# Rows in natural order, one x transfer a group, and an output product merged with the next group's value product in a convolution kernel

## The chip, the cores and the metric

The kernel runs on one core of a Trainium2 chip. The metric is device time in microseconds (us) of one execution; lower is better. A core has five engines that run side by side and wait for one another by semaphores: PE (TensorE, the matmul array, whose weight loads the profile lists as PEld), DVE (VectorE), ACT (ScalarE), POOL (GpSimd) and SP (SyncE). SP and POOL also issue the DMA transfers here; all of these run on the core's 16 DMA engines.

## What is computed

The reference, cut to what matters (batch 8, sequence 4224, 192 channels, 8 heads of 24 channels):

```python
w = softmax(weight_gen)                      # (8, 4224, 8 heads, 7 taps)
x_pad = concat([zeros(8, 6, 192), x], 1)
x_unf = x_pad[:, idx, :].reshape(B, S, 7, 8, 24)
y = einsum('bshk,bskhg->bshg', w, x_unf)     # a convolution with its own 7 taps at every row and head
y = y.reshape(B, S, 192)
gate_pre = sum(conv_w[k] * y_pad[:, k:k + S, :] for k in range(5))   # 5 taps a channel
gate = 1 / (1 + exp(-gate_pre))
out = (gate * (y @ w_val)) @ w_out
```

## The kernel before

**Groups.** The sequence is cut into 36 groups of 118 rows (`BLK`), each for all eight batches. With the rows that the taps reach back to, a group needs 128 rows of x, one for each partition. The per-row convolution is done on PE as a product with a band matrix: for each batch and head the moving operand `tb` holds, in each of the 128 input rows, that row's weights for the output rows it reaches, and the stationary operand is that batch's and head's x. A group goes through these steps:

- `load_x` (L404 to L415): x into `xt`, three buffers. A whole group (all but the first and the last) has eight transfers on POOL's queue, one a batch, 128 rows of 768 bytes each; the first and last group load by chunks of 16 rows on SP's.
- `load_t` (L417 to L424): the softmax weights, which were stored earlier to a DRAM tensor `zd` in a sheared layout, into `tb`, two buffers, in eight chunks of 16 rows on SP's queue. Row r of chunk j lies in partition 8 r + j.
- `bank` (L426 to L441): the convolution, 64 products (128 PE instructions, since each fp32 product takes two passes) on a 32-column split of the array, in four kinds of 16 products, each kind into one PSUM tile `pa`.
- `evac` (L443 to L455): ACT copies `pa` to `A` (channels of four heads a batch), `B` and `S`.
- `move` (L457 to L466): eight small SBUF to SBUF transfers on POOL's queue put the channels of the last two heads from `S` into the holes of `A` (four, L464) and `B` (four, L466).
- `tap0`, `tap`, `sigm` (L472 to L488): the five-tap gate on ACT, DVE and ACT into `aA` and `aB`.
- `val` (L490 to L505): the value product into `v2` (a 64-column split for `A`, L497, then 128 x 128 for `B`, L499) and `v01` (128 x 128, L501, then a split by 64 rows, L504).
- `gv` (L507 to L513): DVE multiplies gate and value in place in `aA`, `aB`.
- `omm` (L515 to L540): the output product, in two halves k = 0, 1, each into the one PSUM tile `po`: a part from `aA` (128 x 128, L524) and one from `aB` (split by 64 rows, L531). Half 0 does the `aB` part first, half 1 the `aA` part.
- `oev` (L542 to L547): ACT copies `po` to `ot`; `store` (L549 to L555): two transfers on SP's queue.

The softmax itself (`Softmax`, L246 to L327) runs in ten parts on DVE and ACT, ahead of the groups that need it, so that it is mixed into about the first two thirds of the groups; its results go to `zd` in transfers of up to 12 rows a partition (L327), from the fourth part on on POOL's queue.

**What sets the order.** Every step is an operation with an engine, an estimated duration, a key (roughly, its due time in groups) and dependencies, added to `Order` (L17 to L86) by `add`. `Order.run` simulates the engines with these estimates and issues on each the open operation with the lowest key among those that could start within `SLACK` of the first. The order that comes out is the instruction order of each engine, and engines and queues go through theirs in order. PE operations carry a `mode` (the shape of the array: "32c", "64c", "64r", "128"); a change of mode costs `SWITCH` in the estimate. `deps` wait for an operation's end; `behind` only fixes the order of issue. The loop over groups (L629 to L700) adds a group's operations: a convolution needs its x and tb, and that the same PSUM buffers were copied out in the group before; the value product needs the moves and that the group before's `gv` is done; an output half needs `gv` and the copying out of the half before it.

Of the kernel before, what the change touches and what calls it, by code (L numbers as in the profile page):

```python
# [7 lines left out]
FP32 = mybir.dt.float32  # L8
# [8 lines left out]
class Order:  # L17
# [1 line left out]


    SLACK = 0.08
    SWITCH = 0.1
    SEM = 0.08
    RATE = 260e3
    LAND = {"SP": 2.8, "ACT": 2.8, "POOL": 3.8}
# [16 lines left out]
    def run(self):  # L42
        for o in self.ops:
            o.left = len(o.deps) + len(o.behind)
            for d in o.deps:
                d.users.append((o, True))
            for d in o.behind:
                d.users.append((o, False))
        free, mode, dma = {}, {}, 0.0
        open_ = {}  # L50
        for n, o in enumerate(self.ops):
            if not o.left:
                open_.setdefault(o.eng, []).append((n, o))
        number = {id(o): n for n, o in enumerate(self.ops)}
        done = 0
        while done < len(self.ops):
            best = None
            for eng, c in open_.items():
                if not c:
                    continue  # L60
                t = free.get(eng, 0.0)
                first = min(max(t, o.ready) for _, o in c)
                n, o = min(((n, o) for n, o in c if max(t, o.ready) <= first + self.SLACK), key=lambda x: (x[1].key, x[0]))
                s = max(t, o.ready)
                if best is None or s < best[0]:
                    best = (s, n, o)
            s, n, o = best
            open_[o.eng].remove((n, o))
            e = s + o.dur
            if o.mode is not None:  # L70
                if mode.get(o.eng, o.mode[0]) != o.mode[0]:
                    e += self.SWITCH
                mode[o.eng] = o.mode[-1]
            free[o.eng] = e
            o.start, o.end = s, e + self.SEM
            if o.bytes:
                dma = max(dma, e + 0.8) + o.bytes / self.RATE
                o.end = dma + self.LAND[o.eng]
# [11 lines left out]
def tile_dynconv_gated_moe(  # L90
# [9 lines left out]
    nc = tc.nc  # L100

    B, S, D = x.shape
# [3 lines left out]
    P = 128  # L106
# [17 lines left out]
    G = 16  # L124
# [255 lines left out]
    class Group:  # L380
# [12 lines left out]

        def rows(self, j):


            lo = FRONT if self.m == 0 and j == 0 else 0
            hi = min(G, self.k - G * j)
            return lo, hi, slice(NGR * lo + j, NGR * (hi - 1) + j + 1, NGR)

        def whole(self):
            return 0 < self.m < NM - 1
# [1 line left out]
        def load_x(self, j):  # L404

            r0 = self.s - FRONT
            if self.whole():
                src = bass.AP(tensor=x.tensor, offset=x.offset + (j * S + r0) * D,
                              ap=[[D, G], [G * D, NGR], [1, D]])
                nc.gpsimd.dma_start(out=self.xb[:, j, 0:D], in_=src)  # L410
# [79 lines left out]
        def val(self):  # L490
            n = HB * self.n
            v2 = self.v2 = ps_v.tile([P, 512], FP32, name="v2")
            v01 = self.v01 = ps_v.tile([P, 2, 512], FP32, name="v01")
            A, Bt = self.part(0, HALO), self.part(1, HALO)
            A = [A[:, HB * u:HB * u + HB] for u in range(2)]
            for u in range(2):
                nc.tensor.matmul(out=v2[HD * u:HD * u + HD, 0:n], lhsT=wvm, rhs=A[u], start=True, stop=False,  # L497
                                 tile_position=(0, HD * u))
            nc.tensor.matmul(out=v2[:, 0:n], lhsT=wvd, rhs=Bt, start=False, stop=True)  # L499
            for u in range(2):  # L500
                nc.tensor.matmul(out=v01[:, u, 0:n], lhsT=wva, rhs=A[u], start=True, stop=False)  # L501
            for u in range(2):
                hs = slice(HD * u, HD * u + HD)
                nc.tensor.matmul(out=v01[:, u, 0:n], lhsT=wvb[hs], rhs=Bt[hs], start=False, stop=True,  # L504
                                 tile_position=(HD * u, 0))  # L505

        def gv(self, g):  # L507
# [7 lines left out]
        def omm(self, k):  # L515

            n = self.n
            po = self.po = ps_o.tile([P, 2, 512], FP32, name="po")

            def a_part(first):  # L520
                for u in range(2):
                    for t in range(2):
                        c = n * (HB * u + 2 * k + t)
                        nc.tensor.matmul(out=po[0:n, u, D * t:D * t + D], lhsT=self.aA[:, c:c + n], rhs=woa,  # L524
                                         start=first and t == 0, stop=not first, skip_group_check=True)

            def b_part(first):
                for t in range(2):
                    for u in range(2):
                        hs, c = slice(HD * u, HD * u + HD), n * (2 * k + t)  # L530
                        nc.tensor.matmul(out=po[0:n, u, D * t:D * t + D], lhsT=self.aB[hs, c:c + n], rhs=wob[hs],  # L531
                                         start=first and t == 0, stop=not first, skip_group_check=True,
                                         tile_position=(HD * u, 0))

            if k == 0:
                b_part(True)
                a_part(False)
            else:
                a_part(True)
                b_part(False)  # L540

        def oev(self, k):  # L542
            if k == 0:
# [65 lines left out]
    def dep(m, name):  # L609
        return T[m][name] if m >= 0 else []  # L610
# [5 lines left out]
    def soft_part(i):  # L616
# [6 lines left out]
        else:  # L623
            softmax(r0, R, at - 5.5, at - 2.2, at - 7.0, at - 1.7)

    for i in range(3):
        soft_part(i)
    late_clear.behind.append(soft[1]["exp"])
    for m, gp in enumerate(gr):  # L629
        if 2 <= m < len(PARTS) - 1:  # L630
# [5 lines left out]
        old = T[m - 3]["bank"] if m >= 3 else [*xpad, xz]  # L636
        late = (() if m == 0 else T[m - 1]["loadt"]) if m < 3 else ()
        d["loadx"] = [add("POOL" if gp.whole() else "SP", 0.55, (-90, -35, -1)[m] if m < 3 else m - 2.2,
                          lambda gp=gp, j=j: gp.load_x(j), old, bytes=G * B * D * 4, behind=late)
                      for j in (range(B) if gp.whole() else gp.chunks)]  # L640
# [49 lines left out]
        d["gv"] = gv  # L690
        d["useA"], d["useB"] = [val, tp[0][-1]], [val, tp[1][-1]]
        o = []
        evs = []
        for k in range(2):
            o.append(add("PE", 6 * mm(D), m + 2.1 + 0.3 * k, lambda gp=gp, k=k: gp.omm(k),
                         [*gv, conv["o"], *(evs[-1:] if k else dep(m - 1, "oev")[-1:])], mode=(("64r", "128"), ("128", "64r"))[k]))
            evs.append(add("ACT", act(4 * D, True), m + 1.2, lambda gp=gp, k=k: gp.oev(k), [o[-1], *(lent("store") if k == 0 else [])]))
        d["out"], d["oev"] = o, evs
        d["store"] = [add("SP", 0.55, m + 2.0, lambda gp=gp, i=i: gp.store(i), evs, delay=4.0,
                          bytes=n * D * 4 * (B if i == 0 else 1)) for i in range(2)]  # L700
    od.run()


# [24 lines left out]
```

## Time and profile before

| | |
|---|---|
| median of 3 runs | 589.19 us |
| lowest, highest | 588.93, 590.83 us |
| the profiled execution's own time | 587.95 us |
| its span in the profile | 586.2 us |
| granted TensorE clock, mean over the span | 0.932 |
| moved by DMA | 123.17 MB in 105869 packets, mean 210 GB/s |

The profile is of one execution. "Busy" is the time in which an engine executes; register, semaphore and DMA-issuing work of a sequencer (SPq, POOLq) is not counted. A row of the timeline gives the start, the length, the engine, the line, the operation, output <- inputs, and how many instructions of this kind in a row (x8); in brackets stands the idle time of the engine before it and what ended it. A row of the groups by line gives the sum of busy time, the mean of one in ns, and the idle time ahead of them with what ended it. The chain that ended last is followed back from the last instruction, at each step to what released it; "issue" is time for which the profile shows no reason. Matmuls overlap with the next one, so that the starts of PE's rows tell more than their lengths. The granted clock is a share of full speed.

### The profile page before, as it was taken

The numbers are of one execution on the slowest core, as the hardware profiler recorded it, in microseconds if no ns is written. First come the engines' busy times: TensorE is split into PE (matmuls) and PEld (weight loads), VectorE is DVE, ScalarE is ACT, GpSimd is POOL, SyncE is SP. The second block draws the span as 40 slices with busy tenths as digits, with TensorE's granted clock in tenths as the row PEclk, the third lists the DMA queues.
The fourth block names the chain that finished last, engine by engine and source line by source line (L and its number), as shares of the span: only waits on it lengthen the run. The fifth ranks groups of instructions, "written<-read, shape, count | busy, mean of one in ns | idle before, by whom it ended". The sixth has DMA issues, their size and how long they took to land.

```text
span 586.2 us, 15839 instructions
## 1 busy us (share of the span) xinstructions
PE 484.9 (83%) x6278; PEld 327.0 (56%) x6278; DVE 438.5 (75%) x488; ACT 345.0 (59%) x533; POOL 330.2 (56%) x613
## 2 busy tenths in 40 slices
PE   2033868599848988999979997998999999999994
PEld 1033535386525764566746673765766675767653
DVE  6776396679857299898887889878975679667780
ACT  4435554478535667458666766586585656546641
POOL 9535956256470666657457455677576687522410
PEclk7557879799987999999979998999999999999999
DMA  5989689738799998879997989799789868775222
GB/s 156 213 239 242 144 223 257 200 99 236 216 236 228 283 266 243 207 207 246 290 259 187 267 217 275 212 261 252 194 217 259 248 158 200 205 183 164 66 60 89
DMA packets 105869, 123.17 MB, mean 210 GB/s; under 512 B 17938, under 2 KB 95615, under 8 KB 103107
## 3 DMA queue, kind: packets, MB, share of 16 engines
q1 hardware_dynamic: 79779, 65.40, 42.5%
q0 software_dynamic: 26016, 56.75, 36.1%
q8 instruction: 50, 0.82, 0.6%
q14 instruction: 24, 0.20, 0.1%
HBM read 64.55 MB, written 51.43 MB: 198 GB/s over the span
## 4 chain that ended last, share of the span: by engine, by line
PE 40%; DMA 30%; POOL 13%; issue 8%; ACT 4%; DVE 2%; SPq 1%; POOLq 0%; ACTq 0%; DVEq 0%
DMA zd<-zt 13%; PE po L524 10%; PE pa L437 10%; POOL xt L410 7%; DMA A<-S 6%; PE po L531 5%; DMA xt<-in_x_dram 5%; PE v L501 5%; DMA tb<-zd 3%; PE v L499 3%; PE v L504 3%; PE v L497 3%; POOL A L464 2%; DMA raw_c<-cd 1%; POOL B L466 1%
## 5 line engine op out<-in xcount | busy, mean ns | idle before, releaser
L483 DVE SCALAR_TENSOR_TENSOR aA<-A,wf,aA 128x944 f32<-128x944 f32 (+1 forms) x144 | 171.6, 1192 | 26.6 <-ACT aA L478 22.8
L437 PE MATMUL pa<-tb,xt 128*32 128x122 f32 (+1 forms) x4608 | 140.5, 276 | 48.8 <-DMA tb<-zd 43.1
L410 POOL DMA_DIRECT2D xt<-in_x_dram x272 | 143.8, 549 | 44.0 <-DMA A<-S 8.7
L437 PEld LDWEIGHTS pa<-tb,xt 128*32 128x32 f32 x4608 | 127.7, 110 | 64.0 <-issue 56.1
L483 DVE SCALAR_TENSOR_TENSOR aB<-B,wf,aB 128x472 f32<-128x472 f32 (+1 forms) x144 | 101.2, 703 | 46.2 <-ACT aB L478 39.0
L466 POOL DMA_DIRECT2D B<-S x144 | 74.7, 525 | 95.8 <-ACT B L451 83.5
L524 PE MATMUL po<-wf,aA 128*118 128x192 f32 (+1 forms) x576 | 117.2, 349 | 11.8 <-DVE aA L511 9.4
L524 PEld LDWEIGHTS po<-wf,aA 128*118 128x118 f32 (+1 forms) x576 | 94.6, 188 | 43.2 <-issue 20.1
L464 POOL DMA_DIRECT2D A<-S x144 | 74.2, 521 | 69.2 <-DMA zd<-zt 36.9
L546 ACT COPY ot<-po 118x768 f32<-118x768 f32 (+1 forms) x72 | 57.8, 803 | 82.3 <-PE po L531 49.4
L531 PE MATMUL po<-wf,aB 64*118 64x192 f32 (+1 forms) x576 | 68.6, 358 | 26.6 <-ACT ot L546 16.8
L531 PEld LDWEIGHTS po<-wf,aB 64*118 64x118 f32 (+1 forms) x576 | 45.8, 183 | 42.6 <-ACT ot L546 18.9
L501 PE MATMUL v<-A,wva 128*128 128x472 f32 (+1 forms) x144 | 63.6, 562 | 0.0
L455 ACT COPY S<-pa 64x488 f32<-64x488 f32 (+1 forms) x72 | 40.5, 562 | 31.1 <-PE pa L437 30.6
L488 ACT ACTIVATE aA<-aA 128x944 f32<-128x944 f32 (+1 forms) x36 | 35.5, 986 | 32.5 <-DVE aA L483 32.5
L511 DVE TENSOR_TENSOR aA<-v,aA 128x944 f32<-128x944 f32 (+1 forms) x36 | 40.7, 1130 | 13.7 <-PE v L504 8.1
L320 ACT COPY zt<-wt 128x192 f32<-128x192 f32 (+3 forms) x100 | 39.1, 461 | 17.5 <-DVE wt L308 11.4
L478 ACT ACTIVATE aA<-A,wf 128x944 f32<-128x944 f32 (+1 forms) x36 | 38.9, 1081 | 14.2 <-DMA A<-S 14.2
L501 PEld LDWEIGHTS v<-A,wva 128*128 128x128 f32 x144 | 27.7, 192 | 31.0 <-issue 30.4
L448 ACT COPY A<-pa 128x488 f32<-128x488 f32 (+1 forms) x72 | 40.5, 565 | 6.5 <-PE pa L437 5.3
L497 PE MATMUL v<-A,wvm 128*64 128x472 f32 (+1 forms) x144 | 38.0, 605 | 7.1 <-DMA A<-S 5.2
L499 PE MATMUL v<-B,wvd 128*128 128x472 f32 (+1 forms) x72 | 39.3, 627 | 0.0
(60 smaller groups left out, 367.5 us busy)
## 6 DMA issues: line engine op xcount, KB each, us to landing
xt<-in_x_dram POOLq DMA_DIRECT2D x272, 96.0 KB, 4.2
tb<-zd SPq DMA_DIRECT2D x285, 88.0 KB
out_dram<-ot SPq DMA_DIRECT2D x35, 672.0 KB
zd<-zt POOLq DMA_DIRECT2D x14, 1104.0 KB, 8.1
wt<-in_weight_gen_dram SPq DMA_DIRECT2D x6, 1120.0 KB
zd<-zt POOLq DMA_DIRECT2D x6, 920.0 KB, 7.5
A<-S POOLq DMA_DIRECT2D x140, 30.5 KB, 4.4
B<-S POOLq DMA_DIRECT2D x140, 15.2 KB, 4.8
```

The costliest lines, as they stand in the source:

```text
L410: nc.gpsimd.dma_start(out=self.xb[:, j, 0:D], in_=src)
L437: nc.tensor.matmul(out=pa[Q * c:Q * c + Q, w * j:w * j + w], lhsT=self.xb[:, u * HB + j, C * h:C * h + Q], rhs=self.t[:, u * HB + j, PAD / ...
L464: nc.gpsimd.dma_start(out=self.A[q:q + n], in_=self.S[p:p + n])
L466: nc.gpsimd.dma_start(out=self.B[HD * u + q:HD * u + q + n], in_=self.S[p:p + n, w * u:w * u + w])
L483: nc.vector.scalar_tensor_tensor(out=a, in0=self.part(g, j), scalar=cw[:, g, j:j + 1], in1=a, op0=ALU.mult, op1=ALU.add)
L497: nc.tensor.matmul(out=v2[HD * u:HD * u + HD, 0:n], lhsT=wvm, rhs=A[u], start=True, stop=False, tile_position=(0, HD * u))
L499: nc.tensor.matmul(out=v2[:, 0:n], lhsT=wvd, rhs=Bt, start=False, stop=True)
L501: nc.tensor.matmul(out=v01[:, u, 0:n], lhsT=wva, rhs=A[u], start=True, stop=False)
L511: nc.vector.tensor_tensor(out=a, in0=self.v01[:, :, 0:n], in1=a, op=ALU.mult)
L524: nc.tensor.matmul(out=po[0:n, u, D * t:D * t + D], lhsT=self.aA[:, c:c + n], rhs=woa, start=first and t == 0, stop=not first, skip_group_ ...
L531: nc.tensor.matmul(out=po[0:n, u, D * t:D * t + D], lhsT=self.aB[hs, c:c + n], rhs=wob[hs], start=first and t == 0, stop=not first, skip_g ...
L546: nc.scalar.copy(out=self.ot[0:n, :, 2 * k:2 * k + 2, :].rearrange("p u t d -> p u (t d)"), in_=self.po[0:n, :, 0:2 * D])
```

## The change

It does five things.

1. Rows in their own order: row r of chunk j lies in partition 16 j + r (`rows`), for x and tb alike. A whole group's x is one transfer on POOL's queue of 128 rows x 8 batches x 768 bytes.
2. The value product `val` is cut in three: `val_c` (the 64-column split into `v2`), `val_a` (the 128 x 128 products for `v2` and `v01`) and `val_b` (the split by 64 rows into `v01`).
3. The output product `omm` is cut into `out_a` and `out_b`, and `output(m, last)` adds one half. The halves of a group's output are no longer added with that group but with the next: the chain of group m on PE is `val_c`, `val_a`, then group m - 1's half 0 (`out_a`, then `out_b`), `val_b`, then half 1 (`out_b`, then `out_a`). `behind` fixes this order. The last group's output follows by itself.
4. A group's convolution is issued behind the last operation of the chain two groups earlier.
5. The planner: `SWITCH` is 0.19, and a change of mode counts already when the next operation is chosen. A chunk of tb is estimated at 0.5 us of SP, a whole x load at 0.55 us of POOL.

```diff
-    SWITCH = 0.1
+    SWITCH = 0.19
...
-                first = min(max(t, o.ready) for _, o in c)
-                n, o = min(((n, o) for n, o in c if max(t, o.ready) <= first + self.SLACK), key=lambda x: (x[1].key, x[0]))
-                s = max(t, o.ready)
+                now = mode.get(eng)
+                at = [(max(t, o.ready), (o.mode is not None and o.mode[0] != now) * self.SWITCH, n, o) for n, o in c]
+                first = min(s + w for s, w, _, _ in at)
+                s, _, n, o = min((a for a in at if a[0] + a[1] <= first + self.SLACK), key=lambda x: (x[3].key, x[2]))
...
-            return lo, hi, slice(NGR * lo + j, NGR * (hi - 1) + j + 1, NGR)
+            return lo, hi, slice(G * j + lo, G * j + hi)
...
-                src = bass.AP(tensor=x.tensor, offset=x.offset + (j * S + r0) * D,
-                              ap=[[D, G], [G * D, NGR], [1, D]])
-                nc.gpsimd.dma_start(out=self.xb[:, j, 0:D], in_=src)
+                src = bass.AP(tensor=x.tensor, offset=x.offset + r0 * D, ap=[[D, P], [S * D, B], [1, D]])
+                nc.gpsimd.dma_start(out=self.xb[:, :, 0:D], in_=src)
...
+        def val_c(self):
+            self.v2 = ps_v.tile([P, 512], FP32, name="v2")
+            for u in range(2):
+                nc.tensor.matmul(out=self.v2[HD * u:HD * u + HD, 0:HB * self.n], lhsT=wvm, rhs=self.rows_of(u),
+                                 start=True, stop=False, tile_position=(0, HD * u))
...
+    def output(m, last):
+        d, gp = T[m], gr[m]
+        n, k = gp.n, len(d.setdefault("oev", []))
+        free = dep(m - 1, "oev")[-1:] if k == 0 else d["oev"][-1:]
+        a, f = m + 2.52 + 0.03 * k, (gp.out_a, gp.out_b)
+        o = [last] if last else []
+        for i, c in enumerate((k, 1 - k)):
+            o.append(add("PE", (4, 2)[c] * mm(D), a + 0.01 * i, lambda c=c, i=i: f[c](k, i == 0),
+                         [d["gv"][1 - c], conv["o"], *(free if i == 0 else [])], mode=(("128",), ("64r",))[c], behind=o[-1:]))
+        lent = dep(m - 3, "store") if m != 2 else [conv["o"], conv["v"]]
+        d["oev"].append(add("ACT", act(4 * D, True), m + 1.2, lambda: gp.oev(k), [o[-1], *(lent if k == 0 else [])]))
+        d["out"] = o[-2:]
+        if k:
+            d["store"] = [add("SP", 0.55, m + 2.0, lambda i=i: gp.store(i), d["oev"], delay=4.0,
+                              bytes=n * D * 4 * (B if i == 0 else 1)) for i in range(2)]
+        return o[-1]
...
-                      for j in (range(B) if gp.whole() else gp.chunks)]
+                      for j in ((0,) if gp.whole() else gp.chunks)]
...
-        d["loadt"] = [add("SP", 0.65, m - 1.8 + 0.01 * j, lambda gp=gp, j=j: gp.load_t(j), [*use, *old],
+        d["loadt"] = [add("SP", 0.5, m - 1.8 + 0.01 * j, lambda gp=gp, j=j: gp.load_t(j), [*use, *old],
...
-                             [*d["loadx"], *d["loadt"], *([x for p_ in prev for x in p_])], mode=("32c",))
+                             [*d["loadx"], *d["loadt"], *([x for p_ in prev for x in p_])], mode=("32c",), behind=dep(m - 2, "last"))
...
-        val = add("PE", 5 * mm(HB * n), m + 1.5, gp.val, [*full[0], *full[1], *placed, *dep(m - 1, "gv")], mode=("64c", "64r"))
-        gv = [add("DVE", dve(size[g]), m + 2.0, lambda gp=gp, g=g: gp.gv(g), [val, sg[g]]) for g in (1, 0)]
+        gv1 = dep(m - 1, "gv")
+        vc = add("PE", mm(HB * n), m + 1.5, gp.val_c, [*full[0], *full[1], *placed, *gv1], mode=("64c",))
+        va = add("PE", 3 * mm(HB * n), m + 1.51, gp.val_a, [*gv1], mode=("128",), behind=[vc])
+        mid = output(m - 1, va) if m else va
+        vb = add("PE", mm(HB * n), m + 1.54, gp.val_b, [], mode=("64r",), behind=[mid])
+        d["last"] = [output(m - 1, vb) if m else vb]
+        d["gv"] = [add("DVE", dve(size[g]), m + 2.0, lambda gp=gp, g=g: gp.gv(g), [(vb, va)[g], sg[g]]) for g in (1, 0)]
+        d["useA"], d["useB"] = [va, tp[0][-1]], [vb, tp[1][-1]]
+    output(NM - 1, output(NM - 1, None))
```

More of the change, by code (lines that the diff above doesn't have):

```diff
@@ L48, in run @@
                 d.users.append((o, False))
-        free, mode, dma = {}, {}, 0.0
+        free, mode, dma = {}, {}, {}
         open_ = {}
@@ L76, in run @@
             if o.bytes:
-                dma = max(dma, e + 0.8) + o.bytes / self.RATE
-                o.end = dma + self.LAND[o.eng]
+                dma[0] = max(dma.get(0, 0.0), e + 0.8) + o.bytes / self.RATE
+                o.end = dma[0] + self.LAND[o.eng]
             o.fn()
@@ L488, in sigm, with rows_of, val_a, val_b @@
             nc.scalar.activation(out=a, in_=a, func=AF.Sigmoid)
-        def val(self):
+        def rows_of(self, u):
+            return self.part(0, HALO)[:, HB * u:HB * u + HB]
+        def val_c(self):
[3 more added lines that the diff above has]
+                                 start=True, stop=False, tile_position=(0, HD * u))
+        def val_a(self):
             n = HB * self.n
[L492 to L495, printed above, removed]
+            nc.tensor.matmul(out=self.v2[:, 0:n], lhsT=wvd, rhs=self.part(1, HALO), start=False, stop=True)
+            self.v01 = ps_v.tile([P, 2, 512], FP32, name="v01")
             for u in range(2):
[L497 to L501, printed above, removed]
+                nc.tensor.matmul(out=self.v01[:, u, 0:n], lhsT=wva, rhs=self.rows_of(u), start=True, stop=False)
+        def val_b(self):
+            Bt = self.part(1, HALO)
             for u in range(2):
                 hs = slice(HD * u, HD * u + HD)
-                nc.tensor.matmul(out=v01[:, u, 0:n], lhsT=wvb[hs], rhs=Bt[hs], start=False, stop=True,
+                nc.tensor.matmul(out=self.v01[:, u, 0:HB * self.n], lhsT=wvb[hs], rhs=Bt[hs], start=False, stop=True,
                                  tile_position=(HD * u, 0))
@@ L513, in gv, with out_a, out_b @@
                 nc.vector.tensor_tensor(out=self.aB, in0=self.v2[:, 0:n], in1=self.aB, op=ALU.mult)
-        def omm(self, k):
+        def out_a(self, k, first):
             n = self.n
-            po = self.po = ps_o.tile([P, 2, 512], FP32, name="po")
-            def a_part(first):
-                for u in range(2):
[L522 to L540, printed above, removed]
+            if first:
+                self.po = ps_o.tile([P, 2, 512], FP32, name="po")
+            for u in range(2):
+                for t in range(2):
+                    c = n * (HB * u + 2 * k + t)
+                    nc.tensor.matmul(out=self.po[0:n, u, D * t:D * t + D], lhsT=self.aA[:, c:c + n], rhs=woa,
+                                     start=first and t == 0, stop=not first, skip_group_check=True)
+        def out_b(self, k, first):
+            n = self.n
+            if first:
+                self.po = ps_o.tile([P, 2, 512], FP32, name="po")
+            for t in range(2):
+                for u in range(2):
+                    hs, c = slice(HD * u, HD * u + HD), n * (2 * k + t)
+                    nc.tensor.matmul(out=self.po[0:n, u, D * t:D * t + D], lhsT=self.aB[hs, c:c + n], rhs=wob[hs],
+                                     start=first and t == 0, stop=not first, skip_group_check=True,
+                                     tile_position=(HD * u, 0))
         def oev(self, k):
@@ L638, in tile_dynconv_gated_moe @@
         d["loadx"] = [add("POOL" if gp.whole() else "SP", 0.55, (-90, -35, -1)[m] if m < 3 else m - 2.2,
-                          lambda gp=gp, j=j: gp.load_x(j), old, bytes=G * B * D * 4, behind=late)
-                      for j in (range(B) if gp.whole() else gp.chunks)]
+                          lambda gp=gp, j=j: gp.load_x(j), old, bytes=(P if gp.whole() else G) * B * D * 4, behind=late)
+                      for j in ((0,) if gp.whole() else gp.chunks)]
         use = [o for a, sts in rows if a < gp.s + n for o in sts] + [front]
         old = dep(m - 2, "bank") if m >= 2 else cleared[m % 2]
-        d["loadt"] = [add("SP", 0.65, m - 1.8 + 0.01 * j, lambda gp=gp, j=j: gp.load_t(j), [*use, *old],
+        d["loadt"] = [add("SP", 0.5, m - 1.8 + 0.01 * j, lambda gp=gp, j=j: gp.load_t(j), [*use, *old],
                           bytes=G * B * RUN * 4) for j in gp.chunks]
@@ L686, in tile_dynconv_gated_moe @@
             sg[g] = add("ACT", act(size[g]), m + 1.9, lambda gp=gp, g=g: gp.sigm(g), [tp[g][-1]])
-        val = add("PE", 5 * mm(HB * n), m + 1.5, gp.val, [*full[0], *full[1], *placed, *dep(m - 1, "gv")], mode=("64c", "64r"))
-        gv = [add("DVE", dve(size[g]), m + 2.0, lambda gp=gp, g=g: gp.gv(g), [val, sg[g]]) for g in (1, 0)]
[L690 to L700, printed above, removed]
+        gv1 = dep(m - 1, "gv")
[7 more added lines that the diff above has]
+    output(NM - 1, output(NM - 1, None))
     od.run()
```

## The prediction

> **What bounds the kernel now.** I read the page first: the span, the slices, the chain that ended last.
>
> ```profile
> span 586.2 us, 15839 instructions
> ...
> PE 484.9 (83%) x6278; PEld 327.0 (56%) x6278; DVE 438.5 (75%) x488; ACT 345.0 (59%) x533; POOL 330.2 (56%) x613
> ...
> PEclk7557879799987999999979998999999999999999
> DMA  5989689738799998879997989799789868775222
> ```
>
> No engine is full over the span, so I cut it into stretches, right behind the value products of groups 3, 22 and 34 (counted by L504 in the timeline), asked for their busy times, and then for the chain inside the middle one.
>
> ```profile
> 0.00:118.40 118.40, 57.00 (x663) 37.93 (x663) 80.64 (x100) 57.67 (x91) 70.27 (x115) 0.75 0.82 207
> 118.40:407.00 288.60, 258.15 (x3437) 173.96 (x3435) 234.32 (x251) 187.92 (x290) 173.40 (x332) 0.96 0.87 236
> 407.00:562.10 155.10, 154.21 (x2091) 104.50 (x2089) 114.69 (x127) 92.86 (x146) 86.49 (x166) 1.00 0.71 184
> 562.10:586.20 24.10, 15.52 (x96) 10.65 (x94) 8.89 (x11) 6.54 (x9) 0.00 (x0) 0.97 0.29 85
> ```
>
> ```profile
> by line: DMA zd<-zt 21.7%; POOL xt L410 13.0%; issue 12.3%; DMA xt<-in_x_dram 10.6%; DMA A<-S 9.7%; PE po L524 5.3%; POOL A L464 3.8%; PE pa L437 3.7%; PE v L501 2.2%; POOL B L466 2.1%; DMA B<-S 1.9%; PE v L497 1.6%; DVE aA L511 1.6%; PE v
> ```
>
> Columns of the stretches: length, busy time of PE, PEld, DVE, ACT and POOL, granted clock, DMA share, GB/s. There are two regimes. In the last 12 full groups (407.00 to 562.10) PE is busy 154.21 of 155.10 us: 12.93 us a group, bound by PE. In the 19 groups of the middle a group takes 288.60 / 19 = 15.19 us, and the chain runs through POOL's queue: the x loads and the waits for x, zd and A transfers. PE is not what binds there: 30 us of it are idle.
>
> The second thing to see is how POOL waits.
>
> ```profile
> 239.77 0.61 POOL L327 DMA_DIRECT2D zd<-zt  x1
> 242.98 2.06 POOL L466 DMA_DIRECT2D B<-S  x4 [2.61 <-ACT B L451]
> 245.04 1.54 POOL L464 DMA_DIRECT2D A<-S  x3
> 247.73 0.52 POOL L464 DMA_DIRECT2D A<-S  x1 [1.16 <-DMA zd<-zt]
> ...
> 297.63 0.55 POOL L327 DMA_DIRECT2D zd<-zt  x1
> 298.22 2.06 POOL L466 DMA_DIRECT2D B<-S  x4
> 300.27 1.54 POOL L464 DMA_DIRECT2D A<-S  x3
> 309.22 0.52 POOL L464 DMA_DIRECT2D A<-S  x1 [7.42 <-DMA zd<-zt]
> 309.84 4.22 POOL L410 DMA_DIRECT2D xt<-in_x_dram  x8
> ```
>
> In both, a zd store is followed by four B moves and three A moves, and the fourth A move, which needs nothing that the third did not, stands until zd has landed. So POOL has eight transfers open at most: a ninth waits for the eighth before it. In the code a group puts eight x loads and eight moves on POOL, and a zd store in most: about 16.6 transfers, so the eight are used up twice in a group.
>
> **The change part by part.** (1) One x transfer for eight. On POOL this takes seven of 16.6 places away, so the eight open transfers reach back most of a group (8 of 9.6) and not half of one. The issue:
>
> ```profile
> L410 POOL DMA_DIRECT2D xt<-in_x_dram x272 | 143.8, 549 | 44.0 <-DMA A<-S 8.7 <-DMA B<-S 8.1 <-issue 5.8
> L199 POOL DMA_DIRECT2D raw_c<-cd x3: 741/774/928, 14.4 to 17.2; - x3
> ...
> xt<-in_x_dram POOLq DMA_DIRECT2D x272, 96.0 KB, 4.2
> zd<-zt POOLq DMA_DIRECT2D x14, 1104.0 KB, 8.1
> ...
> A<-S POOLq DMA_DIRECT2D x140, 30.5 KB, 4.4
> ```
>
> Eight issues take 8 x 0.549 = 4.39 us a group. The new one has 128 x 8 = 1024 runs of 768 B. Below, it costs 0.55 us, as a load of 128 runs does; above, eight times that, 4.39. Nearest are the raw_c loads, which by their shapes have 640 or 320 runs and take 0.74 to 0.93 us: (0.774 - 0.549) / (320 - 128) = 1.2 ns a run, so 0.55 + 896 x 1.2 ns = 1.6 us. I take 1.3, between this and the flat end, so 3.1 us of 4.39 go. On the middle chain "POOL xt" is 13.0% of 288.60 = 37.5 us; 3.1 / 4.39 of that is 26.5 us. The 10.6% (30.6 us) of waits for x to land I count as neither gain nor loss: the new transfer is open for longer (768 KB; between 4.2 us for 96 KB and 8.1 for 1104 KB, so some 7 us), but what stands eight behind it comes nearly a group later. At the ends, all of them go, or as much again is added.
>
> [...]
>
> Where does the stall go? DMA is next: in the middle it is 0.87 busy, so 0.87 x 15.19 = 13.2 us a group if it were never idle and did its work at the same rate. DVE follows with 234.32 / 19 = 12.3. Hence the gain there is at most (15.19 - 13.2) x 19 = 38 us; 26.5 brings a group to 13.8, at a DMA share of 0.96. In the late stretch the same saving lies off the path (POOL is busy 86.49 of 155.10).
>
> (2) Rows in their own order. The products over rows are sums, and the number of runs stays; only where tb's chunks land moves, from every eighth partition to 16 neighbours. SP issues a chunk in about 0.6 us, and it is not the bound:
>
> ```profile
> L424 SPq DMA_DIRECT2D tb<-zd x287: 532/598/3036, 18.5 to 537.2; - x144
> ```
>
> I price this at zero, since chunk j is followed by chunk j + 4 in the other half of the partitions; the other end is a rival below.
>
> (3) The chain on PE. A clean cycle of before:
>
> ```profile
> 426.02 0.91 PE L531 MATMUL po<-wf,aB 64*118 64x192 f32 x8
> 426.87 1.56 PE L524 MATMUL po<-wf,aA 128*118 128x192 f32 x8
> 428.36 1.01 PE L497 MATMUL v<-A,wvm 128*64 128x472 f32 x4
> 429.30 1.06 PE L499 MATMUL v<-B,wvd 128*128 128x472 f32 x2
> 430.20 1.75 PE L501 MATMUL v<-A,wva 128*128 128x472 f32 x4
> 431.88 1.06 PE L504 MATMUL v<-B,wvb 64*128 64x472 f32 x4
> 432.87 1.56 PE L524 MATMUL po<-wf,aA 128*118 128x192 f32 x8
> 434.36 0.91 PE L531 MATMUL po<-wf,aB 64*118 64x192 f32 x8
> 435.20 3.75 PE L437 MATMUL pa<-tb,xt 128*32 128x122 f32 x128
> 438.88 0.91 PE L531 MATMUL po<-wf,aB 64*118 64x192 f32 x8
> ```
>
> 12.86 us, and eight changes of the array's shape: 64 rows, 128, 64 columns, 128, 64 rows, 128, 64 rows, 32 columns. A change costs what a phase takes beyond its passes. Passes of 472 columns start 0.40 us apart:
>
> ```profile
> 429.80 0.56 PE L499 MATMUL v<-B,wvd 128*128 128x472 f32 x1
> 430.20 0.56 PE L501 MATMUL v<-A,wva 128*128 128x472 f32 x1
> ```
>
> The six of L499 and L501 take 431.88 - 429.30 = 2.58 us, 0.18 over 6 x 0.40; the two pairs of L504 take 0.99, 0.19 over; those of L497 0.94, 0.14 over. I take 0.16. The new order is 32 columns, 64 columns, 128 (value and output), 64 rows (output, value, output), 128: five changes. So 3 x 0.16 = 0.48 us go.
>
> It adds a wait. The second output half writes the same po, and must wait for ACT to empty it, with two value passes in between where four or more phases were. With nothing between, this reads:
>
> ```profile
> 563.53 0.91 PE L531 MATMUL po<-wf,aB 64*118 64x192 f32 x8
> 564.49 0.80 ACT L546 COPY ot<-po 118x768 f32<-118x768 f32 x1 [1.90 <-PE po L531]
> 565.34 0.91 PE L531 MATMUL po<-wf,aB 64*118 64x192 f32 x8 [0.90 <-ACT ot L546]
> ```
>
> 0.90 us, of which the two passes of L504 cover 0.80: 0.10 if ACT is free, and up to 0.90 if it has just begun another instruction as long as this one. ACT is busy 92.86 of 155.10 us in 146 instructions, so about 0.60 x 0.4 (a little over half of their mean of 0.64, since long ones are met more often) = 0.25 more. Behind the waiting product stand the rest of the chain and the next convolution. Net: 0.48 - 0.35 = 0.13 us a group, 12 groups: 1.6 us late; at the ends 6 gained (no wait) and 5 lost (a wait of 0.90).
>
> (4) The order by hand: a convolution only after the chain two groups back. Between a group's convolution and its value PE then has the chain before and the convolution behind it, one cycle, 12.86 - 0.48 = 12.4 us. This covers the moves: 2.06 + 1.54 + 0.52 = 4.1 us of issues and 4.4 us of landing (the A<-S row), 8.5. I price it at zero; without the cover it is the rival below. The planner's 0.19 for a change only reorders what is ready; zero as well.
>
> Head: it holds the first of the whole x loads, 3.1 us of POOL each, of which its chain can use part: 2 (0 to 6). Tail: the last output still follows the last value product: 0 (within 2).
>
> Sum: 26.5 + 1.6 + 2 + 0 = 30 us. The profiled execution took 587.95 us, 1.75 beyond its span, and stands 1.24 under the median, 589.19. So 589.19 - 30 = 559.
>
> **The rivals.** *The rigid chain holds output back* (slower). Now PE can do a group's first output (0.85 + 1.49 = 2.34 us) while the next group's moves are under way; afterwards it stands behind the value product. In favour: where zd is ahead, the last A move was issued at 309.22 for a convolution that PE was long done with, and zd keeps its place ahead of the moves. Against: POOL comes to zd and to the moves some 3 us earlier. It decides once moves land over 12.4 us after their convolution. There are 21 zd stores from 76.4 to 451.9:
>
> ```profile
> L327 POOL DMA_DIRECT2D zd<-zt x21: 546/551/606, 76.4 to 451.9; - x21
> ```
>
> By their rate 21 x 288.60 / 375.5 = 16 lie in the middle; 16 x 2.34 = 37 us lost against 30 gained: 596.
>
> *The neighbouring partitions slow the tb loads* (slower). A tb chunk is 88 KB, eight a group; x, out, moves, zd and weights are the rest of 236 GB/s x 15.19 us = 3.58 MB, so tb is 20% of the traffic. If each of its bytes took twice the engine time, 13.2 us of DMA a group would become 15.9, and the middle 19 x (15.9 - 15.19) = 13 us longer, with 4 gained elsewhere: 598. For it: DMA is 0.87 busy. Against: SP issues a chunk every 0.6 us at best, and neighbouring issues go to different halves. [...]
>
> *The zd store goes on holding POOL* (little changes). It is the largest item of the middle chain, 21.7% = 63 us, and the change doesn't touch it. If POOL, relieved of x, only waits longer for zd, the head and the late stretch are what is left: 589 - 4 = 585.
>
> **How the numbers follow.** Chances: the forecast 0.70 with its own range 545 to 578 (x waits of 15 us gone; or a POOL price near the upper end and 0.90 us of po wait), zd holds 0.12, rigid chain 0.11, ports 0.07. The range for 8 in 10 takes in the zd case and leaves the slow ones: 544 to 589. About 0.3%, 1.8 us, is what a measurement here can tell from nothing. Faster: 0.70 and half and more of the zd case, 0.77; same 0.05; slower 0.18.
>
> **What would show it.** Right: "POOL xt" is near 1.3 us an issue, x34, and gone from the middle chain; the middle stretch is near 13.8 us a group with DMA at 0.95 or more; a cycle of late PE has five changes and one wait for ACT ot of 0.1 to 0.5 us before L531; PE's clock stays at 1.0 in the middle. Wrong: the middle still near 15 us with POOL waiting for zd or for x; PE idle ahead of the value product until A<-S lands; L424 issues well over 0.6 us, or a higher DMA share at fewer GB/s; a wait for ACT ot near 1 us in every group.

## The result, and the profile after

The changed kernel takes 563.13 us (median of four runs, 561.0 to 568.36) against 589.08 us before (four runs, 588.93 to 590.83). The ratio is 0.9566, with a 95% interval of 0.9495 to 0.9637. The forecast was 559, in 544 to 589. Here and below a time is the median of all runs of a kernel, while a ratio to the kernel before takes only the runs within 1.5% of their kernel's fastest.

The lines of the page that answer to those of before:

```profile
span 559.2 us, 15347 instructions
...
PE 470.1 (84%) x6278; PEld 328.0 (59%) x6278; DVE 438.8 (78%) x488; ACT 341.7 (61%) x531; POOL 217.6 (39%) x375
...
PEclk9999769999969998999999999999999999999999
DMA  7999958999996999998969999978988899897323
```

POOL has lost a third of its busy time, 330.2 to 217.6 us; unlike those of SP, POOL's DMA issues count as busy in these profiles, and they are the most of it: 31.6 us for x, 74.2 for the B moves and 73.9 for the A moves, 179.7 of the 217.6. The same stretches as before, cut behind the last value products of groups 3, 22 and 34 (L510 now), and the chain inside the middle one:

```profile
0.00:112.40 112.40, 59.29 (x790) 39.46 (x790) 79.96 (x101) 59.25 (x94) 52.73 (x77) 0.92 0.90 210
112.40:382.90 270.50, 245.08 (x3306) 171.84 (x3306) 237.97 (x255) 183.09 (x285) 106.76 (x191) 0.97 0.95 253
382.90:536.10 153.20, 150.50 (x2088) 105.86 (x2088) 112.04 (x123) 91.92 (x145) 58.06 (x107) 1.00 0.80 189
536.10:559.20 23.10, 15.19 (x94) 10.82 (x94) 8.80 (x11) 7.42 (x10) 0.00 (x0) 0.94 0.30 89
```

```profile
by line: PE pa L436 14.7%; PE po L529 12.8%; DMA A<-S 8.1%; PE po L540 7.8%; PE v L504 6.7%; DMA zd<-zt 4.9%; issue 4.8%; ACT ot L548 4.6%; DMA wt<-in_weight_gen_dram 4.4%; PE v L501 4.4%; PE v L496 3.8%; DMA tb<-zd 3.4%; DMA out_dram<-ot 3
```

Of the 27.0 us of span that are gone, 18.1 lie in the middle (288.60 to 270.50, 15.19 to 14.24 us a group), 1.9 in the late stretch, 6.0 ahead of them and 1.0 behind. The issue of x loads (13.0%) and the waits for x (10.6%) are no longer among the leading items of the middle's chain, zd has fallen from 21.7% to 4.9%, and PE's products lead it. DMA is 0.95 busy there.

### The profile page after: what moved, and what is told of

It is laid out like the page before. It is cut to its first block, busy times and chain, and to the rows that moved or that the text cites. A ratio compares the mean times of both kernels' runs of the same rounds, so it can differ in the third digit from the quotient of the medians.

```text
span 559.2 us, 15347 instructions
## 1 busy us (share of the span) xinstructions
PE 470.1 (84%) x6278; PEld 328.0 (59%) x6278; DVE 438.8 (78%) x488; ACT 341.7 (61%) x531; POOL 217.6 (39%) x375
## 4 chain that ended last, share of the span: by engine, by line
PE 52%; DMA 23%; ACT 11%; POOL 5%; DVE 4%; issue 4%; SPq 1%; ACTq 0%; DVEq 0%; POOLq 0%
PE pa L436 14%; PE po L529 13%; PE po L540 8%; DMA A<-S 8%; PE v L504 7%; PE v L501 5%; ACT ot L548 5%; PE v L496 4%; DMA zd<-zt 4%; DMA wt<-in_weight_gen_dram 4%; DMA tb<-zd 3%; DMA B<-S 2%; POOL B L465 2%; ACT S L454 2%; DMA out_dram<-ot 1%
## 5 line engine op out<-in xcount | busy, mean ns | idle before, releaser
L482 DVE SCALAR_TENSOR_TENSOR aA<-A,wf,aA 128x944 f32<-128x944 f32 (+1 forms) x144 | 171.7, 1193 | 26.5 <-ACT aA L477 23.4
L465 POOL DMA_DIRECT2D B<-S x144 | 74.2, 522 | 211.5 <-ACT B L450 209.4
L529 PE MATMUL po<-wf,aA 128*118 128x192 f32 (+1 forms) x576 | 111.1, 337 | 0.9 <-ACT ot L548 0.9
L463 POOL DMA_DIRECT2D A<-S x144 | 73.9, 518 | 53.0 <-DMA zd<-zt 26.7
L540 PE MATMUL po<-wf,aB 64*118 64x192 f32 (+1 forms) x576 | 66.6, 350 | 13.1 <-ACT ot L548 10.2
L540 PEld LDWEIGHTS po<-wf,aB 64*118 64x118 f32 (+1 forms) x576 | 44.3, 178 | 48.4 <-ACT ot L548 40.0
L321 ACT COPY zt<-wt 128x192 f32<-128x192 f32 (+3 forms) x100 | 40.4, 462 | 14.0 <-DVE wt L309 13.5
L409 POOL DMA_DIRECT2D xt<-in_x_dram x34 | 31.6, 928 | 27.6 <-PE po L529 8.9
L501 PE MATMUL v<-B,wvd 128*128 128x472 f32 (+1 forms) x72 | 40.6, 646 | 0.5 <-issue 0.5
```

The costliest lines, as they stand in the source:

```text
L463: nc.gpsimd.dma_start(out=self.A[q:q + n], in_=self.S[p:p + n])
L465: nc.gpsimd.dma_start(out=self.B[HD * u + q:HD * u + q + n], in_=self.S[p:p + n, w * u:w * u + w])
L482: nc.vector.scalar_tensor_tensor(out=a, in0=self.part(g, j), scalar=cw[:, g, j:j + 1], in1=a, op0=ALU.mult, op1=ALU.add)
L501: nc.tensor.matmul(out=self.v2[:, 0:n], lhsT=wvd, rhs=self.part(1, HALO), start=False, stop=True)
L529: nc.tensor.matmul(out=self.po[0:n, u, D * t:D * t + D], lhsT=self.aA[:, c:c + n], rhs=woa, start=first and t == 0, stop=not first, skip_g ...
L540: nc.tensor.matmul(out=self.po[0:n, u, D * t:D * t + D], lhsT=self.aB[hs, c:c + n], rhs=wob[hs], start=first and t == 0, stop=not first, s ...
```

## The experiments

**Which part brings the gain?** The first four kernels take the change apart: the row order, the one x transfer (which is written for that order: in the old one its address pattern would have four dimensions, where the kernel's transfers have three, and it wasn't tried), and the chain on PE with all that belongs to it. With the row order goes the planner's estimate of a tb chunk, 0.5 us for the natural and 0.65 for the old one. The planner makes a new order for each of these kernels, on every engine, so that each difference between them holds what the new order does as well.

`rows_x`: the kernel before with the row order and the one transfer.

```diff
-            return lo, hi, slice(NGR * lo + j, NGR * (hi - 1) + j + 1, NGR)
+            return lo, hi, slice(G * j + lo, G * j + hi)
...
-                nc.gpsimd.dma_start(out=self.xb[:, j, 0:D], in_=src)
+                src = bass.AP(tensor=x.tensor, offset=x.offset + r0 * D, ap=[[D, P], [S * D, B], [1, D]])
+                nc.gpsimd.dma_start(out=self.xb[:, :, 0:D], in_=src)
```

> The kernel before with the natural row order and one x transfer a whole group; PE's order, val and omm, and the choice in the planner as before. Theory P (POOL's eight open places and its issue time were the bound of the middle): nearly all of the gain is here, 589 to about 566 us, the middle near 14.2 us a group, the late stretch unchanged at 12.9. Rival C (the new chain on PE and its order bring the gain): about 584 us.

Measured: 595.14 us, ratio 1.0105 (1.0070 to 1.0139): 1% slower than before.

`rows_only`: the kernel before with the row order alone.

```diff
-            return lo, hi, slice(NGR * lo + j, NGR * (hi - 1) + j + 1, NGR)
+            return lo, hi, slice(G * j + lo, G * j + hi)
...
-                              ap=[[D, G], [G * D, NGR], [1, D]])
+                              ap=[[D, P], [1, D]])
```

> The kernel before with the natural row order alone; x still in eight transfers a group, one a batch, each over 128 neighbouring rows. Theory P: no change, 589 us within 2. Rival R (16 neighbouring partitions speed SP's issues up or slow the landing of tb): 580 or less with SP's tb issues at 0.43 us as the cause, or 595 and more with a higher DMA share.

Measured: 622.8 us, ratio 1.0602 (1.0542 to 1.0662): 35 us slower.

`rows_chain`: the changed kernel with x in eight transfers again.

```diff
-                src = bass.AP(tensor=x.tensor, offset=x.offset + r0 * D, ap=[[D, P], [S * D, B], [1, D]])
-                nc.gpsimd.dma_start(out=self.xb[:, :, 0:D], in_=src)
+                src = bass.AP(tensor=x.tensor, offset=x.offset + (j * S + r0) * D, ap=[[D, P], [1, D]])
+                nc.gpsimd.dma_start(out=self.xb[:, j, 0:D], in_=src)
```

> The changed kernel with x in eight transfers a group again (one a batch). Theory P: the middle goes back to about 15.2 us a group, only the shorter PE cycle of the late stretch stays: about 584 us. Rival C: 566 us or so, as fast as the change nearly.

Measured: 614.15 us, ratio 1.0415 (1.0352 to 1.0478).

`chain_only`: this one with the old row order as well.

```diff
-            return lo, hi, slice(G * j + lo, G * j + hi)
+            return lo, hi, slice(NGR * lo + j, NGR * (hi - 1) + j + 1, NGR)
```

> The changed kernel with the old row order and x in eight transfers: the new chain on PE and the planner alone. Theory P: about 584 us (late stretch 12.75 us a group, middle about 15). Rival C: about 566 us. Rival of the prediction (the rigid chain holds output back): slower than 589, near 596, since POOL is not relieved.

Measured: 592.03 us, ratio 1.0053 (1.0019 to 1.0087).

Ratios to the kernel before, side by side:

| | the old chain | the new chain |
|---|---|---|
| old rows, eight x transfers | 1 | 1.0053 |
| natural rows, eight x transfers | 1.0602 | 1.0415 |
| natural rows, one x transfer | 1.0105 | 0.9566 |

Both theories fall: neither the x transfer nor the chain brings the gain by itself. The row order, with the estimate that goes with it, costs 35 us in the old kernel. The one transfer takes back 0.0497 (29 us) with the old chain and 0.0849 (50 us) with the new one. The new chain gives nothing with the old rows, and 0.0539 (32 us) once x is one transfer. The gain needs both.

**What do the rows cost, and through what?** Section 3 of a page lists the DMA queues, with packets, MB and the time that their packets took as a share of 16 engines' span; q1 is SP's queue, which carries tb, the outputs and the softmax weights. Before:

```profile
q1 hardware_dynamic: 79779, 65.40, 42.5%
```

`rows_only`, with SP's tb issues (shortest, median and longest in ns) under it:

```profile
q1 hardware_dynamic: 79779, 65.40, 46.2%
...
L423 SPq DMA_DIRECT2D tb<-zd x287: 281/429/5247, 18.5 to 575.8; - x144
```

The changed kernel:

```profile
q1 hardware_dynamic: 79779, 65.40, 48.9%
...
L423 SPq DMA_DIRECT2D tb<-zd x287: 281/430/3822, 18.5 to 508.7; - x144
```

The same packets and bytes take 0.425 x 586.2 = 249 us of the 16 engines before, 0.462 x 626.6 = 289 with natural rows alone, and 0.489 x 559.2 = 273 in the changed kernel. Issuing a tb chunk became cheaper at the same time: 430 ns where the prediction's row has 598. In the middle of `rows_only` tb isn't among the leading items of the chain that ended last: the landings of x (16.2%), zd (11.2%), B (10.0%) and A (9.4%) lead it.

Three kernels look for the place. In their traces every engine has its instructions in the same order as in the kernel that they start from, apart from the chunks that `same_ports` swaps, so that here no new order is mixed in. `same_ports` changes only the order in which the changed kernel issues its chunks.

```diff
-            self.chunks = [j for i in range(NGR // 2) for j in (i, i + NGR // 2) if j in c]
+            self.chunks = [j for j in (0, 2, 1, 3, 4, 6, 5, 7) if j in c]
```

> The changed kernel with the tb chunks issued in the order 0, 2, 1, 3, 4, 6, 5, 7, so that chunks next to each other in time lie 32 partitions apart and not 64. [...]

Measured: 566.81 us, ratio 0.9603 (0.9534 to 0.9671), which overlaps the change's. SP's queue takes 0.495 x 564.0 = 279 us, for 273. Which chunks follow one another makes no difference to the time that these runs show.

`tb_old_rows` is the changed kernel with tb alone in the old partitions.

```diff
             lo, hi, p = self.rows(j)
+            p = slice(NGR * lo + j, NGR * (hi - 1) + j + 1, NGR)
             c0 = G // 2 * j * CELL
```

> The changed kernel, but the tb chunks go to the old partitions (8 r + j) while x stays in the natural order with one transfer. The convolution then pairs rows wrongly, so its values are not the reference's; the instructions, their shapes and bytes are the change's. Theory T (the natural order costs because a tb chunk's 16 neighbouring partitions take each of the DMA engines longer): the SP queue's engine time falls from 0.489 x 559 = 273 us to about 250, SP's issues go back to 0.6 us, and the time falls to about 545. Rival X (the order of x's rows is what costs): 563, no change.

Measured: 560.98 us, ratio 0.9532 (0.9498 to 0.9567). The row of SP's queue and of its issues, span 559.9 us:

```profile
q1 hardware_dynamic: 79779, 65.40, 44.4%
...
L424 SPq DMA_DIRECT2D tb<-zd x287: 532/598/3971, 18.5 to 510.6; - x144
```

0.444 x 559.9 = 249 us: the engine time is back at that of before, and so are the 598 ns. So it is where tb's chunks land that costs 25 us of the engines. Yet the time is the change's within the intervals, and not the 545 us that Theory T gave: in the changed kernel these 25 us are hidden.

`x_new_rows` is the kernel before with x alone in the natural order, in eight transfers.

```diff
-                              ap=[[D, G], [G * D, NGR], [1, D]])
+                              ap=[[D, P], [1, D]])
...
+                p = slice(G * j + lo, G * j + hi)
                 src = bass.AP(tensor=x.tensor, offset=x.offset + (r0 + G * j + lo) * D,
```

> The kernel before, but x in the natural order, still in eight transfers, while tb keeps its old partitions; here too the convolution pairs rows wrongly and only the time is read. Theory T: 588, the SP queue's engine time stays at 250 us. Rival X: most of the 35 us that both orders together cost, 610 to 623.

Measured: 591.26 us, ratio 1.0038 (1.0008 to 1.0067). So hardly 2 of the 35 us come from x, and SP's queue takes 0.435 x 583.5 = 254 us. Theory T holds for the place where the engines lose time, tb. For the 33 us that are left it isn't shown: `rows_only` differs from this kernel in where tb lands and in the estimate of 0.5 us, and its trace has another order on every engine (PE's differs in 22 of the 36 groups). No run has tb's new rows in the old order, so tb's slower landing and the new order are two candidates, and neither is excluded. For the landing speaks the pair `chain_only` and `rows_chain`: PE's order differs there in three groups only, and 0.0362 (21 us) lie between them, at 251 and 284 us of SP's queue; the other engines' orders differ in more places.

**What of the chain brings the gain?** `eight_changes` turns the two parts of each output half around, so that PE changes the array's shape eight times a group again.

```diff
-        for i, c in enumerate((k, 1 - k)):
+        for i, c in enumerate((1 - k, k)):
```

> The changed kernel with the two parts of each output half in the other order, so that the array's shape changes eight times a group again while all else stays. By the prediction's 0.16 us a change, 0.48 us a group where PE binds: 12 groups late make 6 us, and up to 12 more in the rest: 569 to 581 us. Rival (the changes are hidden behind other waits): 563.

Measured: 579.69 us, ratio 0.9777 (0.9696 to 0.9859), 0.0211 or 12.4 us above the change. Three changes in each of 36 groups are 108: 0.115 us each, if nothing else that the other order moves counts. That is not certain: the planner also shifts some quarters of convolutions in this kernel. The run shows that the kernel with more changes takes 12.4 us longer; what PE does in a change is in no row.

`free_bank` drops the rule that a convolution comes only behind the chain two groups back.

```diff
-                             [*d["loadx"], *d["loadt"], *([x for p_ in prev for x in p_])], mode=("32c",), behind=dep(m - 2, "last"))
+                             [*d["loadx"], *d["loadt"], *([x for p_ in prev for x in p_])], mode=("32c",))
```

> The changed kernel without the rule that a convolution is issued only behind the chain two groups back. Theory A (the strict alternation keeps PE's order steady where the planner's estimates are off, and is a part of the gain): slower, 570 to 580. Rival B (the rule only takes freedom away, as the prediction's slower rival had it): 558 or less. If the planner would have alternated anyway: 563.

Measured: 596.13 us, ratio 1.0123 (1.0064 to 1.0183): 33 us above the change, and above the kernel before too. Without it the chain gives nothing at all. The programs show what the rule does to PE's order, with c for a quarter of a convolution and V for a value product. The kernel before, the change, and `free_bank`, from the first group on:

```
before     ccccccccVcccccccVcVVccccccccVcccccccVcVVccccccccVcccccccVccVcccVccccVccccVccccVccccVccccV...
the change ccccccccVccccVccccVVccccccccVccccVccccVVccccccccVccccVccccVccccVccccVccccVcccVcccccVccccV...
free_bank  ccccccccVccccccccVVVccccccccccccVVccccVVccccccccVccccccccVVccccVVccccccccccVcccccVcVcccVcccccV...
```

The kernel before sets nearly all its convolutions in pairs for its first ten groups and alternates from then on, but for one pair late; the change has a pair once in four groups there, and then none; `free_bank` goes on pairing. The starts of each group's last value product in the timelines show where this tells:

| us a group | groups 3 to 10 | groups 10 to 22 | groups 22 to 34 |
|---|---|---|---|
| before | 16.95 | 14.17 | 12.92 |
| the change | 14.87 | 13.87 | 12.77 |
| `free_bank` | 16.19 | 16.12 | 13.20 |
| `chain_only` | 17.76 | 14.43 | 12.80 |
| `rows_x` | 16.41 | 15.65 | 13.21 |

7 x 2.08 = 14.6 of the 18.1 us that the middle gained lie in groups 3 to 10, where the order of before is paired and that of the change mostly isn't. `chain_only` has the alternation but neither the x transfer nor the row order, and loses there: the alternation alone isn't enough. From the trace of `free_bank` the middle, its chain, and rows of PE and SP:

```profile
107.67:414.44 306.77, 255.18 (x3437) 179.19 (x3436) 243.41 (x262) 194.00 (x304) 108.88 (x196) 0.94 0.91 232
```

```profile
by line: PE pa L436 13.4%; DMA tb<-zd 12.8%; PE po L529 12.3%; DMA A<-S 8.2%; PE po L540 7.4%; PE v L504 5.7%; SPq L557 4.4%; issue 4.3%; ACT ot L548 3.9%; PE v L496 3.7%; PE v L501 3.6%; SPq L423 3.6%; DMA xt<-in_x_dram 3.3%; DVE aA L482 1
```

```profile
240.90 1.56 PE L529 MATMUL po<-wf,aA 128*118 128x192 f32 x8
242.39 1.01 PE L496 MATMUL v<-A,wvm 128*64 128x472 f32 x4
...
247.21 3.81 PE L436 MATMUL pa<-tb,xt 128*32 128x122 f32 x122
252.50 0.43 PE L436 MATMUL pa<-tb,xt 128*32 128x122 f32 x6 [1.47 <-issue]
...
252.97 4.60 SPq L423 DMA_DIRECT2D tb<-zd  x8
...
257.00 3.74 PE L436 MATMUL pa<-tb,xt 128*32 128x122 f32 x128
268.01 3.48 PE L436 MATMUL pa<-tb,xt 128*32 128x122 f32 x64 [7.28 <-issue]
271.42 1.84 PE L496 MATMUL v<-A,wvm 128*64 128x472 f32 x4
```

Left free, the planner lets two chains follow one another (242.39 comes straight behind the last output of the chain before) and then sets convolutions close together: 247, 257 and half of the next at 268, with PE idle for 7.28 us between, for which the profile names no reason. tb has two buffers, and the loads of tb are 12.8% of this middle's chain, 3.4% of the change's. SP issues eight loads of tb from 252.97 on, as soon as the convolution of 247 is done with its buffer. That pairs cost because both tb buffers come free, and must be filled, at once is argued from these rows and not shown; the run itself shows what the rule is worth. Why `rows_x` is slow in groups 10 to 22 too stays open: its order goes on setting convolutions close together up to its 14th value product, and the slower tb loads and the eight changes of shape are in it as well.

`old_planner` takes back the choice and its constant.

```diff
-    SWITCH = 0.19
+    SWITCH = 0.1
...
-                at = [(max(t, o.ready), (o.mode is not None and o.mode[0] != now) * self.SWITCH, n, o) for n, o in c]
+                at = [(max(t, o.ready), (o.mode is not None and o.mode[0] != now) * 0.0, n, o) for n, o in c]
```

> The changed kernel with SWITCH 0.1 again and a choice of the next operation that doesn't count the change of shape. The prediction's zero for this part: 563 within 2. Rival S (the choice keeps the chain's products of one shape together, and is part of the gain): PE's cycle has more than five changes, 568 to 580.

Measured: 578.41 us, ratio 0.9744 (0.9682 to 0.9806), 10 us above the change. Its interval doesn't overlap the change's, so the planner's choice and its constant are part of the gain. It isn't the shape changes that they save: PE's instructions in the traces have 193 of them in place of 183, about 1 us at 0.115 us each. What in the new order costs the rest stays open.

**What holds POOL now?** Two kernels try to take more from POOL's eight places. `zd_act` issues the zd stores from ACT:

```diff
-            q = QUEUES[0 if len(soft) < 3 else 2]
+            q = QUEUES[0 if len(soft) < 3 else 1]
```

> The changed kernel with the zd stores of parts 3 to 9 issued from ACT and not from POOL. Theory P2 (the places that zd takes on POOL hold the A moves, 24 us of waits in the middle): about 550 us, the middle near 13.6 us a group. Rival D (DMA, 0.95 busy in the middle, is the bound now): 560 or more.

Measured: 612.02 us, ratio 1.0327 (1.0254 to 1.0400). The time rose by 45 us. Theory P2 misses, and Rival D's "560 or more" covers it without a reason for so much. The edit did free the places: POOL's A moves wait 26.7 us for zd in the change's trace, and in this one no wait of POOL for zd is among the larger ones. Something dearer came in; whether the stores hold ACT up or the order that the planner makes of them does is open, so the run doesn't say what POOL's places are worth.

`x_late` issues x behind the moves:

```diff
-        d["loadx"] = [add("POOL" if gp.whole() else "SP", 0.55, (-90, -35, -1)[m] if m < 3 else m - 2.2,
+        d["loadx"] = [add("POOL" if gp.whole() else "SP", 0.55, (-90, -35, -1)[m] if m < 3 else m - 1.6,
```

> The changed kernel with the x load's key at m - 1.6 and not m - 2.2, so that it is issued behind the moves of the group that frees its buffer and not ahead. Theory P2: the third A move no longer stands until x has landed (14 us of waits in the middle): about 555 us. Rival D: 561 to 563. If x now lands too late for its convolution: slower, with PE waiting for xt.

Measured: 571.28 us, ratio 0.9722 (0.9668 to 0.9775), 9 us slower than the change. The chain of its middle:

```profile
by line: DMA A<-S 14.9%; PE pa L436 12.5%; PE po L529 12.4%; DMA tb<-zd 12.4%; PE po L540 7.7%; PE v L504 6.7%; DMA B<-S 4.6%; PE v L501 4.2%; ACT ot L548 4.2%; PE v L496 4.1%; issue 3.7%; POOL B L465 2.0%; POOL A L463 1.7%; ACT zt L321 1.7
```

x isn't among its leading items, so it is not x that comes too late, and neither are the waits for zd; the landing of the A moves and of tb has taken their place. But the edit did little of what it was meant for. In the middle POOL's A moves still wait 11.9 us for x (14.3 in the change), 15.7 for zd (24.4) and 12.3 for B moves (5.6), 39.9 in all in place of 44.3. So this run doesn't decide between the theories either, and what bounds the middle now stays open.

## Why the prediction was right in its number, and where its reasons failed

The size, 30 us forecast and 26 measured, was near. That owes much to luck, for the sum behind it was not right. Going from before to the change by way of `rows_only` and `rows_x`, the steps are +35 us for the rows, -29 for the one transfer and -32 for the chain with the planner. Two of the parts priced at zero are each worth more than the whole gain, with opposite signs.

**Part 2, the rows, priced at zero.** This step failed for the kernel before: there the rows, with their estimate, cost 35 us, while SP's queue takes 289 in place of 249 us of the engines. The prediction's own rival for it, with a chance of 0.07 and a price of 13 us, had the mechanism of slower landing, and `tb_old_rows` confirms that for the engine time. The doubling of tb's engine time that its price assumes no run shows; SP's whole queue takes 273 us against 249 with the chunks put back, a tenth more. How much of the 35 us is the landing and how much the new order that the estimate makes stays open. In the changed kernel the zero held for tb, since `tb_old_rows` gives the same time within the intervals; but not for the prediction's reason, that chunk j is followed by chunk j + 4 in the other half, as `same_ports` shows. The engines did take longer, and it was hidden.

**Part 4, the order by hand, priced at zero, with a slower rival.** This step failed in sign. The prediction took the rule as a loss of freedom, covered. Without the rule the time is 33 us higher. The cover, 12.4 us for 8.5 us of moves, was a fair reading of a kernel that alternates; what was missed is that the kernel before doesn't in its first ten groups, and that the rule takes most of the pairs away just where 14.6 us of the gain lie. Why pairs cost is argued above, not shown. The timeline of before had them to be seen.

**Part 1, the x transfer.** The places and the issue were read rightly, the sum was not what the runs give: the middle gained 18.1 us, not 26.5. The issue takes 0.93 us (1.3 predicted, 0.55 to 4.39 as bounds), the landing 8.4 (7 predicted):

```profile
L409 POOL DMA_DIRECT2D xt<-in_x_dram x34 | 31.6, 928 | 27.6 <-PE po L529 8.9
...
xt<-in_x_dram POOLq DMA_DIRECT2D x34, 768.0 KB, 8.4
zd<-zt POOLq DMA_DIRECT2D x14, 1104.0 KB, 10.4
```

That POOL holds eight transfers shows again, with x now as one of those that hold:

```profile
142.30 0.93 POOL L409 DMA_DIRECT2D xt<-in_x_dram  x1 [3.99 <-PE pa L436]
143.22 0.55 POOL L328 DMA_DIRECT2D zd<-zt  x1
144.41 2.07 POOL L465 DMA_DIRECT2D B<-S  x4 [0.63 <-ACT B L450]
146.47 1.03 POOL L463 DMA_DIRECT2D A<-S  x2
154.08 0.52 POOL L463 DMA_DIRECT2D A<-S  x1 [6.58 <-DMA xt<-in_x_dram]
156.86 0.52 POOL L463 DMA_DIRECT2D A<-S  x1 [2.25 <-DMA zd<-zt]
```

The third A move is the eighth behind x and waits 6.58 us for it, the fourth waits 2.25 us for zd. So the waits for x were not gone, as the prediction's end for a full gain had it, nor doubled. The 26.5 us were ascribed to POOL alone; the runs show 29 us for the one transfer against the rows that it needs, and 50 with the new chain. The middle came to 14.24 us a group, not 13.8, at the forecast DMA share of 0.95. PE's clock there was 0.97; the prediction's "stays at 1.0" misread its own row of before, which has 0.96.

**Part 3, the chain on PE.** This is the step that held. A clean cycle:

```profile
411.20 3.76 PE L436 MATMUL pa<-tb,xt 128*32 128x122 f32 x128
414.89 1.01 PE L496 MATMUL v<-A,wvm 128*64 128x472 f32 x4
415.84 1.06 PE L501 MATMUL v<-B,wvd 128*128 128x472 f32 x2
416.74 1.75 PE L504 MATMUL v<-A,wva 128*128 128x472 f32 x4
418.32 1.46 PE L529 MATMUL po<-wf,aA 128*118 128x192 f32 x8
419.71 0.91 PE L540 MATMUL po<-wf,aB 64*118 64x192 f32 x8
420.46 0.96 PE L510 MATMUL v<-B,wvb 64*128 64x472 f32 x4
421.52 0.91 PE L540 MATMUL po<-wf,aB 64*118 64x192 f32 x8
422.37 1.56 PE L529 MATMUL po<-wf,aA 128*118 128x192 f32 x8
423.86 3.74 PE L436 MATMUL pa<-tb,xt 128*32 128x122 f32 x128
```

12.66 us for 12.86, with five changes of shape: 0.20 us gained, 0.13 predicted. The value product L510 stands for 1.06 us where its two pairs of passes take 0.80: the wait for `ot` is 0.26, predicted 0.35. Without the wait the three changes would have gained 0.20 + 0.26 = 0.46 us, 0.15 each, so the 0.16 that was taken holds where PE binds; the 0.115 us from `eight_changes` is a mean over all groups. The late stretch gained 1.9 us (1.6 predicted). But the 12.4 us of `eight_changes` are more than even 12 x 0.46 = 5.5 us for the late groups: the changes, or what moved with them, count ahead of the late stretch too, which the sum left out, since it held PE not to bind there.

**The planner, priced at zero**, is worth 10 us; this step failed too. **The head** gained 6 us, the upper end of its bounds, the tail 1; no run shows by what.

## What to carry to other kernels

Where several resources are each near their limit, the parts of a change need not add (here +35, -29 and -32 us): price them in the combination that will run, and run the combinations before believing in a part, since a step priced at zero can be worth more than the one that the forecast rests on. An order that looks like lost freedom can be the gain: look in the timeline whether an engine's large steps alternate or come in pairs. Where a planner makes the order, compare the orders of two kernels before ascribing their difference to the edit, since one estimate can move every engine's. And when a layout is changed to make one transfer simpler, ask what it does to the other transfers that must follow that layout.

## What the runs showed of the hardware that was not expected

The same 287 chunks of 16 rows take SP 598 ns to issue into every eighth partition and 430 ns into 16 neighbouring ones, and take the DMA engines longer in the second case: 273 us for all of SP's queue in the changed kernel, 249 with these chunks alone put back (`tb_old_rows`), at the same order of every engine. The cheaper issue comes with the dearer transfer. On POOL, an issue of 1024 runs of 768 bytes takes 928 ns, one of 128 such runs 549: 0.42 ns a run.
